# An attention and two-layer kernel: fewer transfers for q, k and v, left over rows placed on both sides

## The chip, the core and the metric

The kernel runs on one core of a Trainium2 chip. The core has five engines that run on their own and meet by semaphores: TensorE (PE; its weight loads are PEld), VectorE (DVE), ScalarE (ACT), GpSimd (POOL) and SyncE (SP), which here only issues transfers. Each engine takes its instructions in order. SBUF and PSUM are the on-chip memories, with 128 partitions; TensorE writes to PSUM only. The metric is the device time of one execution, in microseconds (us).

## The reference, cut to what matters

```python
batch, n_heads, seq, head_dim = (4, 8, 576, 64)
scores = scale * np.matmul(q, k.transpose(0, 1, 3, 2))
thresh = np.max(scores, axis=-1, keepdims=True) - tau
scores = np.where(scores >= thresh, scores, -1000000000.0)
attn = np.exp(scores - np.max(scores, axis=-1, keepdims=True))
attn = attn / (np.sum(attn, axis=-1, keepdims=True) + 1e-09)
x = np.matmul(attn, v)                 # then (2304, 512): tokens by heads
r = np.maximum(x @ w_in, 0.0)          # layer one, 512 -> 2048 -> 512
x = (s * (r * r) + b) @ w_out
h = x @ w2_in                          # layer two, 512 -> 2048 -> 512
out = (h * np.tanh(softplus(h))) @ w2_out
```

All is in float32. There are 32 heads; the kernel takes them as 16 pairs.

## The kernel before, in words

**Attention by pairs.** A pair of heads has 2 x 576 rows of q, k and v. `load_raw` brings them to SBUF: partition p holds rows 4p to 4p+3 of the first 512, as four chunks, and the 64 left over rows lie in a fifth chunk, in half of the partitions. For the second head the order is shifted for k and v, so that its left over rows come first. `prep_qk` transposes the five chunks of both heads at once on TensorE (L204) into a PSUM tile tp; the same tiles hold the scores. ScalarE copies it to `hi` in a rounded format (L208), VectorE makes `lo`, the rest (L209), and `move` brings both to the tiles Q, KH and KL, in which each head owns one half of the partitions and the other half holds the counterpart or zeros (L226; in the first pair engines do it). `hi` and `lo` have one buffer each, so the next hi waits until the moves out of it have landed. Right after the transpositions the raw tile is filled again for the next pair.

A pair's scores come in nine steps: four of head 0, one with the left over rows of both, four of head 1. A step is S (L252), the negated scores and their minimum ns (L256), the threshold (L258), the exponentials e (L263), masking and row sums (L267), scaling (L277). Seven steps later e is transposed (T, L289 to L298), copied to te (L300), and multiplied with v (pv, L311). At a pair's end `split_x` makes xh and xl. The T of the left over columns is made by two ordinary products with 64 columns of the identity (L297, L298).

**The layers.** Layer one (`moe1`) takes the tokens of four pairs as one block. Its products (L403) need weights split in two parts. `split_w` does that by pieces of 256 KB: a load into one of three raw buffers (L57), a scaling on ScalarE (L62), three passes on VectorE (L64 to L66; the last frees the raw buffer), a copy on ScalarE (L69), a subtraction on GpSimd (L70). Two pieces make a unit, of which five fit in the ring; units of block 0 are stored to DRAM (L107), and the other blocks load them whole (L395). Layer two (`moe2`) follows when all attention is done.

**What sets the order.** The program makes attention steps until four pairs are ready, with one step of weight splitting in each twelve. Then `run` hands out steps of attention and of layer one in proportion to what is left of each, attention at a higher priority. A list scheduler with its own model of durations turns this into one order for each engine. SyncE issues nearly all transfers, in that order, and a transfer that waits holds up those behind it.

The lines that the change touches most, of the loads of k and of the moves of q:

```python
nc.sync.dma_start(t[:, 0:4, 0, :], h2[0, 0:512, :].rearrange("(p c) d -> p c d", c=4))
full = h2[1, 64:576, :].rearrange("(p c) d -> p c d", c=4)
nc.sync.dma_start(t[64:128, 0:4, 1, :], full[0:64])
nc.sync.dma_start(t[0:64, 1:5, 1, :], full[64:128])
parts = [(Q, 0, 576, 0)] if h == 0 else [(Q, 0, 512, 704), (Q, 512, 576, 128)]
```

## Time and profile before

| | |
|---|---|
| median of 3 runs | 1206.59 us (1204.57 to 1207.52) |
| profiled execution | 1204.01 us |
| its span, first to last instruction | 1201.8 us |
| PE busy | 1145.2 us, 95% |
| DVE, ACT, POOL busy | 626.1, 529.7, 427.3 us |
| mean granted clock | 0.991 |
| transfers | 161.84 MB, 123667 packets |

The span is one execution on the chip. Busy time is the time in which an engine has an instruction at work; matmuls overlap, so a busy TensorE is not one at its peak. A wait is put down to what came last. Releasers in brackets say what ended an engine's idle time. "issue" is a wait for something that the profile does not show.

### The profile page before, as it was taken

The numbers are of one execution on the slowest core, as the hardware profiler recorded it, in microseconds if no ns is written. First come the engines' busy times: TensorE is split into PE (matmuls) and PEld (weight loads), VectorE is DVE, ScalarE is ACT, GpSimd is POOL, SyncE is SP. The second block draws the span as 40 slices with busy tenths as digits, with TensorE's granted clock in tenths as the row PEclk, the third lists the DMA queues.
The fourth block names the chain that finished last, engine by engine and source line by source line (L and its number), as shares of the span: only waits on it lengthen the run. The fifth ranks groups of instructions, "written<-read, shape, count | busy, mean of one in ns | idle before, by whom it ended". The sixth has DMA issues, their size and how long they took to land.

```text
span 1201.8 us, 19799 instructions
## 1 busy us (share of the span) xinstructions
PE 1145.2 (95%) x7104; PEld 979.2 (81%) x7104; DVE 626.1 (52%) x1505; ACT 529.7 (44%) x1073; POOL 427.3 (36%) x600
## 2 busy tenths in 40 slices
PE   4888999898899999999999999999999999999998
PEld 4666888877678998988988999878888888888886
DVE  5888777878885464655552689964111111111111
ACT  4666666575655544445533465553221221222211
POOL 4566777776644334326422344432000000000000
PEclk8989999999999999999999999999999999999999
DMA  5657466576595455374423898763030020030000
GB/s 128 166 136 183 110 217 184 159 207 173 170 289 156 158 154 159 125 233 140 136 86 106 256 324 283 276 230 105 1 105 1 1 70 1 1 105 1 19 1 35
DMA packets 123667, 161.84 MB, mean 135 GB/s; under 512 B 57393, under 2 KB 78897, under 8 KB 123569
## 3 DMA queue, kind: packets, MB, share of 16 engines
q1 hardware_dynamic: 123568, 160.58, 43.5%
q8 instruction: 56, 0.92, 0.3%
q14 instruction: 43, 0.34, 0.1%
HBM read 107.48 MB, written 30.93 MB: 115 GB/s over the span
## 4 chain that ended last, share of the span: by engine, by line
PE 69%; DMA 10%; DVE 8%; POOL 5%; issue 3%; ACT 2%; SPq 2%; DVEq 0%; ACTq 0%; POOLq 0%
PE o L522 17%; PE h L403 11%; PE y L403 10%; PE hm L493 8%; PE hp L493 8%; PE pv L311 6%; DMA wraw<-in_moe_w_in_dram 4%; PE S L252 4%; DMA wraw<-in_moe_w_out_dram 4%; PE T L289 3%; POOL e L277 3%; DVE wa L64 1%; DMA w<-w 1%; DVE wa L65 1%; DVE wa L66 1%
## 5 line engine op out<-in xcount | busy, mean ns | idle before, releaser
L507 DVE TENSOR_TENSOR g2l<-t,g2h 128x512 fp32r<-128x512 f32 (+1 forms) x80 | 51.9, 648 | 315.4 <-ACT t L506 311.6
L403 PE MATMUL y<-gh,w 128*128 128x288 f32 x768 | 164.6, 300 | 3.1 <-DVE y L450 2.9
L403 PE MATMUL h<-xh,w 128*128 128x288 f32 x768 | 165.5, 301 | 1.9 <-DMA w<-w 1.7
L522 PE MATMUL o<-w2o,g2h 128*128 128x512 f32 x576 | 150.0, 395 | 1.9 <-ACT g2h L505 1.9
L267 DVE SCALAR_TENSOR_TENSOR e<-ns,st,e 128x576 f32<-128x576 f32 x128 | 119.2, 935 | 47.3 <-ACT e L263 33.4
L277 POOL TENSOR_SCALAR e<-e,st 128x576 f32<-128x576 f32 x128 | 127.5, 1005 | 32.3 <-DVE st L272 26.1
L256 DVE TENSOR_SCALAR_CACHE_REDUCE ns<-S 128x576 f32<-128x576 f32 x144 | 107.7, 751 | 54.2 <-PE S L252 53.3
L403 PEld LDWEIGHTS y<-gh,w 128*128 128x128 f32 x768 | 125.8, 188 | 11.1 <-issue 4.4
L403 PEld LDWEIGHTS h<-xh,w 128*128 128x128 f32 x768 | 125.9, 188 | 9.5 <-issue 5.7
L263 ACT ACTIVATE e<-ns,st 128x576 f32<-128x576 f32 x128 | 98.8, 776 | 70.9 <-DVE ns L256 59.6
L522 PEld LDWEIGHTS o<-w2o,g2h 128*128 128x128 f32 x576 | 107.0, 188 | 26.7 <-ACT g2h L505 2.3
L300 ACT COPY te<-T 128x576 f32<-128x576 f32 x144 | 91.1, 632 | 66.6 <-PE T L294 60.5
L258 POOL TENSOR_SCALAR st<-st,tau_c 128x1 f32<-128x1 f32 x144 | 61.1, 426 | 164.9 <-DVE ns L256 140.7
L403 PE MATMUL y<-gl,w 128*128 128x288 f32 x384 | 113.8, 297 | 0.5 <-DVE gl L427 0.5
L252 PE MATMUL S<-KH,Q 128*128 128x288 f32 x320 | 100.3, 329 | 14.6 <-DVE ns L256 5.0
L403 PE MATMUL h<-xl,w 128*128 128x288 f32 x384 | 113.8, 297 | 0.0
L289 PE MATMUL T<-ident,e 128*128 128x128 f32 x576 | 98.3, 279 | 13.8 <-ACT te L300 8.6
L493 PE MATMUL hm<-y,w2i 128*128 128x512 f32 (+1 forms) x480 | 108.4, 372 | 0.0
L493 PE MATMUL hp<-y,w2i 128*128 128x512 f32 (+1 forms) x480 | 107.2, 372 | 0.0
L427 POOL TENSOR_TENSOR gl<-rr,gh 128x288 fp32r<-128x288 f32 x96 | 80.6, 845 | 73.8 <-DVE rr L426 63.2
L311 PE MATMUL pv<-te,rawv 128*64 128x288 f32 x640 | 105.6, 420 | 0.0
L493 PEld LDWEIGHTS hm<-y,w2i 128*128 128x128 f32 x480 | 84.5, 188 | 18.0
(94 smaller groups left out, 2122.7 us busy)
## 6 DMA issues: line engine op xcount, KB each, us to landing
w<-w SPq DMA_DIRECT2D x96, 512.0 KB, 4.2
wraw<-in_moe_w_in_dram SPq DMA_DIRECT2D x64, 256.0 KB, 3.9
w<-wp SPq DMA_DIRECT2D x32, 512.0 KB, 4.0
wraw<-in_moe_w_out_dram SPq DMA_DIRECT2D x64, 256.0 KB, 4.4
KH<-hik SPq DMA_DIRECT2D x60, 144.0 KB, 2.5
y<-yT SPq DMA_DIRECT2D x32, 256.0 KB, 4.0
KL<-lok SPq DMA_DIRECT2D x30, 144.0 KB, 2.7
rawq<-in_q_dram SPq DMA_DIRECT2D x32, 128.0 KB, 3.0
```

Of the source, the lines that this page charges most:

```text
L252: nc.tensor.matmul(so, Q[:, c0:c0 + 128], kt[:, ks], start=(i == 0), stop=(i == len(terms) - 1))
L256: nc.vector.tensor_scalar(ns.rearrange("p (h n) -> p h n", h=2), sv, -0.125, 3.0e38, op0=ALU.mult, op1=ALU.min, accum_out=nm[:, c1])
L263: nc.scalar.activation(e, ns, AF.Exp, bias=nm[:, c1], scale=-1.0)
L267: nc.vector.scalar_tensor_tensor(e, ns, nthr[:, c1], e, op0=ALU.is_le, op1=ALU.mult, accum_out=sm[:, c1])
L277: nc.gpsimd.tensor_scalar(t, t, rinv[:, j:j + 1], u[:, j:j + 1], op0=ALU.mult, op1=ALU.add)
L289: nc.tensor.transpose(T[:, i * 128:i * 128 + 128], self.es[pr, i, "pair"][:, o:o + 128], self.ident)
L300: nc.scalar.copy(te, T[:, :576])
L311: self.nc.tensor.matmul(self.pv[HALVES[h], hf * HB:hf * HB + 288], v[:, h, c, :], tes[h][:, hf * 288:hf * 288 + 288], start=first, stop=last)
L403: nc.tensor.matmul(acc[:, :n], w[:, wl, c], rhs[c][xl][:, ts], start=(i == 0), stop=(i == 11))
L427: (nc.vector if b == 3 else nc.gpsimd).tensor_tensor(gl[:, ts], r2, gh[:, ts].bitcast(F32), op=ALU.subtract)
L493: nc.tensor.matmul(hp[:, :n], w[:, wl, kc, fs], yy[kc], start=(i == 0), stop=(i == 11))
L522: nc.tensor.matmul(outs[t], g[:, t * 128:t * 128 + 128], w[:, wl, fc % 4, :], start=(fc == 0 and i == 0), stop=(fc == 15 and i == 2))
```

## The change

The loads of a pair take 7 transfers: for q and for k one for the first 512 rows of both heads and one for the left over rows, for v one and two. No order is shifted any more. Instead `raw_t` places the transposed left over rows twice in tp, before the other chunks (columns 192 to 256) and behind them (768 to 832), by two ordinary products with 64 columns of the identity; hi and lo are 640 columns wide, head 0 uses the columns from 64 on and head 1 those up to 576. So each move is one piece: 6 for k and 4 for q, 10 in place of 12. In the first pair `prep_first` gives hi and lo of q tiles of their own, copies the parts of head 0 on three engines, and moves those of head 1 by transfers; q's first load is issued on ScalarE. The zeros of the raw tiles are written earlier, and the small constants share one tile.

```diff
@@ -36,11 +36,9 @@
         self.ident, self.swap = i2[:, 0:128], i2[:, 64:192]
         make_identity(nc, self.ident)
         nc.gpsimd.tensor_copy(i2[:, 128:192], i2[:, 0:64])
-        self.tau_c = pool.tile([P, 1], F32, name="tau_c")
-        self.s_c = pool.tile([P, 1], F32, name="s_c")
-        self.b_c = pool.tile([P, 1], F32, name="b_c")
-        self.colsum = pool.tile([P, 4], F32, name="colsum")
-        self.cb = pool.tile([P, 4], F32, name="cb")
+        small = pool.tile([P, 11], F32, name="small")
+        self.tau_c, self.s_c, self.b_c = (small[:, i:i + 1] for i in range(3))
+        self.colsum, self.cb = small[:, 3:7], small[:, 7:11]
 
 
     def split_w(self, src, hi, lo, pool, tags, kw):
@@ -132,6 +130,10 @@
     def attn_alloc(self):
         nc = self.nc
         self.sets = []
+        self.qk = {}
+        for n in "kq":
+            t = self.qk[n] = self.at.tile([P, 5, 2, 64], F32, name=f"raw{n}", bufs=1)
+            nc.gpsimd.memset(t[64:128, 4], 0.0)
 
         e4 = self.at.tile([P, 1344], F32, name="E4", bufs=1)
         for g in range(3):
@@ -146,10 +148,6 @@
             for h in range(2):
                 nc.gpsimd.memset(KL[h][HALVES[1 - h], :].bitcast(F32), 0.0)
             self.sets.append((Q, KH, KL, e4[:, g * 640:g * 640 + 704]))
-        self.qk = {}
-        for n in "qk":
-            t = self.qk[n] = self.at.tile([P, 5, 2, 64], F32, name=f"raw{n}", bufs=1)
-            nc.gpsimd.memset(t[64:128, 4], 0.0)
         self.vs = []
         for g in range(2):
             t = self.at.tile([P, 2, 5, 64], F32, name=f"rawv{g}", bufs=1)
@@ -163,28 +161,19 @@
         if b >= self.B:
             return
         src = {"q": self.q, "k": self.k, "v": self.v}[nm]
+        dma = nc.scalar if nm == "q" and not pr else nc.sync
         h2 = src[b, 2 * p:2 * p + 2]
-        rem = h2[:, 512:576, :].rearrange("h r d -> r h d")
+
+        most = h2[:, 0:512, :].rearrange("h (p c) d -> p c h d", c=4)
         if nm == "v":
             t = self.vs[pr % 2]
+            nc.sync.dma_start(t[:, :, 0:4, :], most.rearrange("p c h d -> p h c d"))
             for h in range(2):
-                nc.sync.dma_start(t[:, h, 0:4, :], h2[h, 64 * h:64 * h + 512, :].rearrange("(p c) d -> p c d", c=4))
-            nc.sync.dma_start(t[0:64, 0, 4, :], h2[0, 512:576, :])
-            nc.sync.dma_start(t[64:128, 1, 4, :], h2[1, 0:64, :])
+                nc.sync.dma_start(t[HALVES[h], h, 4, :], h2[h, 512:576, :])
         else:
             t = self.qk[nm]
-            nc.sync.dma_start(t[:, 0:4, 0, :], h2[0, 0:512, :].rearrange("(p c) d -> p c d", c=4))
-            if nm == "q":
-                nc.sync.dma_start(t[:, 0:4, 1, :], h2[1, 0:512, :].rearrange("(p c) d -> p c d", c=4))
-                nc.sync.dma_start(t[0:64, 4, :, :], rem)
-            else:
-
-
-                full = h2[1, 64:576, :].rearrange("(p c) d -> p c d", c=4)
-                nc.sync.dma_start(t[64:128, 0:4, 1, :], full[0:64])
-                nc.sync.dma_start(t[0:64, 1:5, 1, :], full[64:128])
-                nc.sync.dma_start(t[0:64, 0, 1, :], h2[1, 0:64, :])
-                nc.sync.dma_start(t[0:64, 4, 0, :], h2[0, 512:576, :])
+            dma.dma_start(t[:, 0:4], most)
+            dma.dma_start(t[0:64, 4, :, :], h2[:, 512:576, :].rearrange("h r d -> r h d"))
         self.raws[pr, nm] = t
 
     def s_tile(self, name):
@@ -193,43 +182,64 @@
         pool = self.s2p if self.s2p and self.n_s % 2 else self.sp
         return pool.tile([P, 1024], F32, tag="S", name=name)
 
+    def raw_t(self, pr, n):
+        nc = self.nc
+        raw = self.raws.pop((pr, n))
+        tp = self.s_tile(f"tp{n}{pr}")
+
+        for c, o in ((4, 192), (0, 256), (1, 384), (2, 512), (3, 640), (4, 768)):
+            rows = raw[:, c].rearrange("p h d -> p (h d)")
+            if c < 4:
+                nc.tensor.transpose(tp[:, o:o + 128], rows, self.ident)
+            else:
+                nc.tensor.matmul(tp[:, o:o + 64], rows, self.ident[:, 0:64], start=True, stop=True)
+        self.load_raw(pr + 1, n)
+        return tp
+
+    def parts(self, pr, n, tp, tags):
+        nc = self.nc
+        hi, lo = (self.at.tile([P, 1152 if t == "e" else 640], F32R, tag=t, name=f"{w}{n}{pr}",
+                               bufs=8 if t == "e" else 1)[:, :640] for w, t in zip(("hi", "lo"), tags))
+        nc.scalar.copy(hi, tp[:, 192:832])
+        nc.vector.tensor_tensor(lo, tp[:, 192:832], hi.bitcast(F32), op=ALU.subtract)
+        return hi, lo
+
+    def moves(self, pr, n, h, hi, lo):
+
+
+        Q, KH, KL, _ = self.sets[pr % 2]
+        own, oth = HALVES[h], HALVES[1 - h]
+        cols = slice(64 - 64 * h, 640 - 64 * h)
+        out = []
+        for half, t in ((own, hi), (oth, hi if n == "k" else lo)):
+            dst = KH[h] if n == "k" else Q[:, 640 * h:640 * h + 576]
+            out.append((dst[half, :], t[own, cols]))
+        return out + ([(KL[h][own, :], lo[own, cols])] if n == "k" else [])
+
     def prep_qk(self, pr, n):
 
-
-        nc = self.nc
-        raw = self.raws.pop((pr, n))
-        Q, KH, KL, _ = self.sets[pr % 2]
-        tp = self.s_tile(f"tp{n}{pr}")
-        for c in range(5):
-            nc.tensor.transpose(tp[:, c * 128:c * 128 + 128], raw[:, c].rearrange("p h d -> p (h d)"), self.ident)
-        self.load_raw(pr + 1, n)
-        hi = self.at.tile([P, 576], F32R, tag="hi", name=f"hi{n}{pr}", bufs=1)
-        lo = self.at.tile([P, 576], F32R, tag="lo", name=f"lo{n}{pr}", bufs=1)
-        nc.scalar.copy(hi, tp[:, :576])
-        nc.vector.tensor_tensor(lo, tp[:, :576], hi.bitcast(F32), op=ALU.subtract)
-        for h, (own, oth) in enumerate((HALVES, HALVES[::-1])):
-            for half, t in ((own, hi), (oth, hi if n == "k" else lo)):
-                if n == "k":
-                    parts = [(KH[h], 0, 576, 0)]
-                else:
-                    parts = [(Q, 0, 576, 0)] if h == 0 else [(Q, 0, 512, 704), (Q, 512, 576, 128)]
-                for dst, a, z, o in parts:
-                    self.move(pr, dst[half, a + o:z + o], t[own, a:z], t is hi)
-            if n == "k":
-                self.move(pr, KL[h][own, :], lo[own, :], None)
-
-    def move(self, pr, dst, src, early):
-
-
-        nc = self.nc
-        if pr:
-            nc.sync.dma_start(dst.bitcast(F32), src.bitcast(F32))
-        elif early is None:
-            nc.gpsimd.tensor_copy(dst, src.bitcast(F32))
-        elif early and dst.shape[-1] > 64:
-            nc.scalar.copy(dst, src.bitcast(F32))
-        else:
-            nc.vector.tensor_copy(dst, src.bitcast(F32))
+        hi, lo = self.parts(pr, n, self.raw_t(pr, n), ("hi", "lo"))
+        for h in range(2):
+            for dst, src in self.moves(pr, n, h, hi, lo):
+                self.nc.sync.dma_start(dst.bitcast(F32), src.bitcast(F32))
+
+    def prep_first(self):
+
+
+        nc = self.nc
+        tps = [self.raw_t(0, n) for n in "kq"]
+        (kh, kl), (qh, ql) = (self.parts(0, n, tp, tags) for n, tp, tags in
+                              zip("kq", tps, (("hi", "lo"), ("e", "e"))))
+        k0, k1, k2 = self.moves(0, "k", 0, kh, kl)
+        q0, q1 = self.moves(0, "q", 0, qh, ql)
+        nc.scalar.copy(k0[0], k0[1].bitcast(F32))
+        nc.gpsimd.tensor_copy(k1[0], k1[1].bitcast(F32))
+        nc.gpsimd.tensor_copy(k2[0], k2[1].bitcast(F32))
+        nc.scalar.copy(q0[0], q0[1].bitcast(F32))
+        nc.vector.tensor_copy(q1[0], q1[1].bitcast(F32))
+        for n, hi, lo in (("k", kh, kl), ("q", qh, ql)):
+            for dst, src in self.moves(0, n, 1, hi, lo):
+                nc.sync.dma_start(dst.bitcast(F32), src.bitcast(F32))
 
 
 
@@ -334,8 +344,7 @@
         nc.sync.dma_start(self.s_c, self.s.partition_broadcast(P))
         nc.sync.dma_start(self.b_c, self.b.partition_broadcast(P))
         self.load_raw(0, "v")
-        for n in "kq":
-            self.prep_qk(0, n)
+        self.prep_first()
         fin = todo = None
         tes = {}
         for k in range(N + LAG + 2):
```

Three places of the order that the scheduler makes of it. First ScalarE at the start of the program, before (hik, hiq: the copies to hi of pair 0; KH, Q: the tiles of the scores; e: exponentials; in brackets the semaphores waited for):

```order
L208 CAST hik0_165<-tpk0_154 128x576 [waits PE_49]
L230 CAST KH00_115<-hik0_165 64x576 [waits Activation_49]
L230 CAST KH00_115<-hik0_165 64x576
L230 CAST KH01_116<-hik0_165 64x576 x2
L208 CAST hiq0_184<-tpq0_175 128x576 [waits DVE_49,PE_49,Activation_49]
L230 CAST Q0_113<-hiq0_184 64x576 [waits Activation_49]
L230 CAST Q0_113<-hiq0_184 64x512
L263 ACTIVATE e0_0_203<-ns0_0_200,st0_194 128x576 [waits DVE_49]
L263 ACTIVATE e0_1_213<-ns0_1_210,st0_194 128x576 [waits DVE_49]
```

And with the change (wraw0: the first raw piece of the weights, wp: its split result):

```order
L175 DMA rawq_107<-in_q_dram 128x8x64
L176 DMA rawq_107<-in_q_dram 64x2x64
L203 ACT_TABLE_LOAD
L203 CAST hik0_163<-tpk0_145 128x640 [waits PE_49]
L235 CAST KH00_115<-hik0_163 64x576 [waits Activation_49]
L60 ACTIVATE wraw0_335<-wraw0_335 128x256 [waits DMAHW2_49]
L203 CAST hiq0_167<-tpq0_154 128x640 [waits PE_49]
L238 CAST Q0_113<-hiq0_167 64x576 [waits Activation_49]
L67 CAST wp0_0_0_334<-wa0_337 128x256 [waits DVE_49]
L273 ACTIVATE e0_0_190<-ns0_0_187,st0_181 128x576 [waits DVE_49]
```

The loads of q stand at the head of ScalarE's queue, two moves of KH01 are gone, and the scaling of the first weight piece has come to stand ahead of hiq.

Second, SyncE where pair 8's k is prepared and pair 9's loaded, before (rawk, rawv: loads; hik, lok: the sources of moves; w1: a store of a weight unit):

```order
L186 DMA rawk_131<-in_k_dram 64x64
L176 DMA rawk_131<-in_k_dram 128x4x64
L184 DMA rawk_131<-in_k_dram 64x4x64
L185 DMA rawk_131<-in_k_dram 64x4x64
L187 DMA rawk_131<-in_k_dram 64x64
L226 DMA KH00_115<-hik8_2876 64x576 x2
L226 DMA KL00_117<-lok8_2877 64x576
L226 DMA KH01_116<-hik8_2876 64x576 x2
L226 DMA KL01_118<-lok8_2877 64x576
L172 DMA rawv0_133<-in_v_dram 64x64
L173 DMA rawv0_133<-in_v_dram 64x64
L107 DMA w1_0_2_3_3156<-wp0_2_3_2980 128x1024
```

And with the change (wraw: loads of weight pieces 44 and 45):

```order
L55 DMA wraw44_3182<-in_moe_w_out_dram 128x2x256
L175 DMA rawk_105<-in_k_dram 128x8x64
L176 DMA rawk_105<-in_k_dram 64x2x64
L224 DMA KH00_115<-hik8_2826 64x576 x2
L224 DMA KL00_117<-lok8_2827 64x576
L224 DMA KH01_116<-hik8_2826 64x576 x2
L224 DMA KL01_118<-lok8_2827 64x576
L172 DMA rawv0_129<-in_v_dram 64x64 x2
L105 DMA w1_0_3_0_3176<-wp0_3_0_3023 128x1024
L55 DMA wraw45_3220<-in_moe_w_out_dram 128x2x256
```

Five loads of k have become two, the six moves are as before, and loads of weights stand directly before and close behind.

Third, TensorE in block 0, where output group (2, 1) of layer one is made (y0_2_1_0 and y0_2_1_1 are its two halves, gh and gl the hidden values, wp1_2_1 the weight unit), before, between the scores S8_1 and S8_2:

```order
L403 MATMUL y0_2_1_0_3756<-gh0_2_0_2708,wp1_2_1_3306 128x288
L403 MATMUL y0_2_1_0_3756<-gl0_2_0_2709,wp1_2_1_3306 128x288
L403 MATMUL y0_2_1_1_3803<-gh0_2_0_2708,wp1_2_1_3306 128x290
L403 MATMUL y0_2_1_1_3803<-gl0_2_0_2709,wp1_2_1_3306 128x290
L403 MATMUL y0_2_1_0_3756<-gh0_2_0_2708,wp1_2_1_3306 128x288
L403 MATMUL y0_2_1_0_3756<-gh0_2_1_2817,wp1_2_1_3306 128x288
L403 MATMUL y0_2_1_0_3756<-gl0_2_1_2818,wp1_2_1_3306 128x288
L403 MATMUL y0_2_1_0_3756<-gh0_2_1_2817,wp1_2_1_3306 128x288
L403 MATMUL y0_2_1_1_3803<-gh0_2_0_2708,wp1_2_1_3306 128x290
L403 MATMUL y0_2_1_1_3803<-gh0_2_1_2817,wp1_2_1_3306 128x290
L403 MATMUL y0_2_1_1_3803<-gl0_2_1_2818,wp1_2_1_3306 128x290
L403 MATMUL y0_2_1_1_3803<-gh0_2_1_2817,wp1_2_1_3306 128x290
```

And with the change, between T7_2 and the other half:

```order
L412 MATMUL y0_2_1_0_3699<-gh0_2_0_2660,wp1_2_1_3254 128x288
L412 MATMUL y0_2_1_0_3699<-gl0_2_0_2661,wp1_2_1_3254 128x288
L412 MATMUL y0_2_1_0_3699<-gh0_2_0_2660,wp1_2_1_3254 128x288
L412 MATMUL y0_2_1_0_3699<-gh0_2_1_2769,wp1_2_1_3254 128x288
L412 MATMUL y0_2_1_0_3699<-gl0_2_1_2770,wp1_2_1_3254 128x288
L412 MATMUL y0_2_1_0_3699<-gh0_2_1_2769,wp1_2_1_3254 128x288
L412 MATMUL y0_2_1_0_3699<-gh0_2_2_3203,wp1_2_1_3254 128x288
L412 MATMUL y0_2_1_0_3699<-gl0_2_2_3204,wp1_2_1_3254 128x288
L412 MATMUL y0_2_1_0_3699<-gh0_2_2_3203,wp1_2_1_3254 128x288
L412 MATMUL y0_2_1_0_3699<-gh0_2_3_3292,wp1_2_1_3254 128x288
L412 MATMUL y0_2_1_0_3699<-gl0_2_3_3293,wp1_2_1_3254 128x288
L412 MATMUL y0_2_1_0_3699<-gh0_2_3_3292,wp1_2_1_3254 128x288
```

The twelve products of a half, which stood in pieces of two and four, now stand in one run, ahead of pair 8's scores rather than among them.

## Rows read from the trace of the kernel before

**Rows 1.** Busy us by stretch: PE, PEld, DVE, ACT, POOL; clock, DMA:
```profile
0.00:31.00 31.00, 15.40 (x63) 12.86 (x64) 16.65 (x45) 13.80 (x21) 15.81 (x50) 0.87 0.54 127
31.00:131.00 100.00, 87.69 (x566) 63.98 (x565) 83.06 (x237) 63.15 (x110) 60.70 (x84) 0.94 0.59 158
131.00:354.00 223.00, 206.57 (x1469) 176.29 (x1467) 176.83 (x440) 137.57 (x288) 161.84 (x227) 1.00 0.63 187
354.00:660.00 306.00, 305.26 (x2251) 272.90 (x2252) 162.52 (x393) 145.74 (x271) 121.91 (x172) 1.00 0.49 150
```

**Rows 2.** SyncE's queue, what it waited for, 131 to 354: us, times, longest:
```profile
SPq L57 <- DVE wa L66: 53.1, 21, 6.2
SPq L186 <- PE tpk L204: 12.6, 4, 8.6
SPq L176 <- PE tpq L204: 9.4, 3, 4.0
```

**Rows 3.** Timeline of SyncE's queue, 186 to 204 us: start, us, instruction:
```profile
192.04 0.61 SPq L186 DMA_DIRECT2D rawk<-in_k_dram  x1
...
201.55 1.29 SPq L57 DMA_DIRECT2D wraw<-in_moe_w_out_dram  x2
```

**Rows 4.** Timeline of VectorE, 192.5 to 193.2 us:
```profile
192.19 0.78 DVE L66 SCALAR_TENSOR_TENSOR wa<-wraw,wa 128x256 int32<-128x256 int32 x1
```

**Rows 5.** Timeline of TensorE, 108 to 122 us:
```profile
116.45 0.33 PE L297 MATMUL T<-ident,E 128*128 128x64 f32 x2
116.62 0.39 PE L298 MATMUL T<-ident,E 128*128 128x64 f32 x2
116.84 0.72 PE L204 MATMUL tpq<-ident,rawq 128*128 128x128 f32 x5
```

**Rows 6.** Busy time of line L208 alone by stretch: us, ACT (count):
```profile
131.00:354.00 223.00, 6.33 (x10) 1.00 0.63 187
354.00:660.00 306.00, 6.32 (x10) 1.00 0.49 150
```

**Rows 7.** Timeline of all engines, 0 to 24 us:
```profile
0.72 0.70 SPq L176 DMA_DIRECT2D rawk<-in_k_dram  x1
...
5.32 1.30 PE L204 MATMUL tpk<-ident,rawk 128*128 128x128 f32 x5 [5.32 <-DMA rawk<-in_k_dram]
...
8.09 1.30 PE L204 MATMUL tpq<-ident,rawq 128*128 128x128 f32 x5 [1.47 <-DMA rawq<-in_q_dram]
...
10.07 0.64 ACT L208 CAST hiq<-tpq 128x576 fp32r<-128x576 f32 x1
...
12.36 0.58 PE L252 MATMUL S<-KH,Q 128*128 128x288 f32 x1 [2.97 <-DVE Q L232]
...
18.29 0.43 ACT L62 ACTIVATE wraw<-wraw 128x256 f32<-128x256 f32 x1 [2.05 <-DMA wraw<-in_moe_w_in_dram]
```

**Rows 8.** DMA issues: size and median us from issue to landing:
```profile
wraw<-in_moe_w_in_dram SPq DMA_DIRECT2D x64, 256.0 KB, 3.9
...
rawq<-in_q_dram SPq DMA_DIRECT2D x32, 128.0 KB, 3.0
```

**Rows 9.** VectorE by line, 31 to 131 us: busy us, mean ns, idle:
```profile
L66 DVE SCALAR_TENSOR_TENSOR wa<-wraw,wa 128x256 int32<-128x256 int32 x11 | 5.6, 512 | 0.1
L65 DVE SCALAR_TENSOR_TENSOR wa<-wraw,wa 128x256 int32<-128x256 int32 x11 | 5.0, 456 | 0.0
L64 DVE TENSOR_SCALAR wa<-wraw 128x256 int32<-128x256 int32 x11 | 4.2, 389 | 1.9 <-POOL wp L70 1.3 <-ACT wraw L62 0.5
```

**Rows 10.** ScalarE, what it waited for, 0 to 131: us, times, longest:
```profile
ACT wraw L62 <- DMA wraw<-in_moe_w_in_dram: 6.0, 5, 2.1
...
ACT hiq L208 <- issue: 1.6, 1, 1.6
```

**Rows 11.** Groups of ScalarE and of VectorE, 131 to 354 us:
```profile
L319 ACT CAST xh<-pv 128x576 fp32r<-128x576 f32 x6 | 3.8, 633 | 0.5 <-PE pv L311 0.5
...
L320 DVE TENSOR_TENSOR xl<-pv,xh 128x576 fp32r<-128x576 f32 x6 | 4.5, 748 | 0.4 <-ACT xh L319 0.4
```

More of the change, by code (lines that the diff above doesn't have):

```diff
@@ L194, in s_tile @@
         return pool.tile([P, 1024], F32, tag="S", name=name)
-    def prep_qk(self, pr, n):
+    def raw_t(self, pr, n):
         nc = self.nc
         raw = self.raws.pop((pr, n))
-        Q, KH, KL, _ = self.sets[pr % 2]
-        tp = self.s_tile(f"tp{n}{pr}")
-        for c in range(5):
-            nc.tensor.transpose(tp[:, c * 128:c * 128 + 128], raw[:, c].rearrange("p h d -> p (h d)"), self.ident)
-        self.load_raw(pr + 1, n)
-        hi = self.at.tile([P, 576], F32R, tag="hi", name=f"hi{n}{pr}", bufs=1)
-        lo = self.at.tile([P, 576], F32R, tag="lo", name=f"lo{n}{pr}", bufs=1)
-        nc.scalar.copy(hi, tp[:, :576])
-        nc.vector.tensor_tensor(lo, tp[:, :576], hi.bitcast(F32), op=ALU.subtract)
-        for h, (own, oth) in enumerate((HALVES, HALVES[::-1])):
-            for half, t in ((own, hi), (oth, hi if n == "k" else lo)):
-                if n == "k":
-                    parts = [(KH[h], 0, 576, 0)]
-                else:
-                    parts = [(Q, 0, 576, 0)] if h == 0 else [(Q, 0, 512, 704), (Q, 512, 576, 128)]
-                for dst, a, z, o in parts:
-                    self.move(pr, dst[half, a + o:z + o], t[own, a:z], t is hi)
-            if n == "k":
-                self.move(pr, KL[h][own, :], lo[own, :], None)
@@ new lines, in prep_qk @@
+    def prep_qk(self, pr, n):
+        hi, lo = self.parts(pr, n, self.raw_t(pr, n), ("hi", "lo"))
[3 more added lines that the diff above has]
+    def prep_first(self):
+        nc = self.nc
+        tps = [self.raw_t(0, n) for n in "kq"]
[11 more added lines that the diff above has]
+                nc.sync.dma_start(dst.bitcast(F32), src.bitcast(F32))
```

## The prediction

> **What bounds the kernel now.** I read the busy time by stretch first [rows 1]. Four stretches matter. Up to 31 us one pair of heads starts up; from 31 to 131 us attention runs alone; from 131 to 354 us attention and the first block of layer one share the machine, and that block's weights are split on the way in; from 354 to 660 us attention and blocks 1 and 2 run on weights that are already split. In the last of these TensorE is busy 305.26 of 306 us: what is added there is paid in full. From 131 to 354 it lacks 16.4 us (223 less 206.57), with VectorE at 79%. From 31 to 131 it lacks 12.3 us, VectorE has 83%, and the granted clock is 0.94. So a gain can come only from about 16 us in the third stretch, some of 12 in the second and 15.6 in the first; the rest of the program can only lose.
>
> Next I asked what SyncE's queue waits for from 131 to 354 us [rows 2]: 53.1 us at the weight load (L57) for a raw buffer to be read out, 22.0 us at loads of k and q for the transposes before them. The queue is in order, so the weight loads stand behind the attention's transfers. The timeline shows one such place [rows 3]: VectorE's pass that frees a raw weight buffer ends at 192.97 [rows 4], but the load that reuses a buffer is issued at 201.55, because from 192.04 on five loads of k, six moves and what stands beside them are issued first, some 0.6 us each. There are two such bursts in each pair.
>
> **The change, part by part.** All sums are against the profiled execution: 1204.0 us, span 1201.8. The median of the runs shown is 1206.6, so 2.6 us are added at the end.
>
> *The spare columns on TensorE.* Before, a raw tile of q or k takes five transpositions. Five of them take 0.72 us with the tail of the last, about 0.27 [rows 5], so one costs 0.11. Now four remain, and the left over rows go through two ordinary products with 64 columns of the identity. The trace has this form: the products of T at L297 and L298, each recorded as two instructions. They start at 116.45 and 116.62, and the next work at 116.84: 0.39 us for two. A tile costs 4 x 0.11 + 0.39 = 0.83 us against 0.55: 0.28 us more, on 32 tiles 9.0 us. The copies to hi tell where the tiles lie [rows 6]: ten fall from 354 us on, where TensorE never idles: +2.8 us, paid. Ten fall in the weight stretch: 2.8, half hidden, +1.4. Twelve (3.4 us) fall before, where other engines set the pace; they are in the prologue's term. The bounds: if the two products cost no more than two transpositions, 3.5 us in all; at a fallen clock the difference can be half as much again.
> The Trainium skill, "TensorE: Matmul & The Clock Gate", section Terms, speaks against this part: it says transpose mode is 4 times faster for fp32. By that rule two 64-column products cost as much as four transpositions, 0.44 us, and the sum would be 10.6 us in place of 9.0. The rows say 3.5 times, and they decide.
>
> *Wider copies.* The copy to hi (ScalarE) and the subtraction (VectorE; 0.75 us for the same form in [rows 11]) grow from 576 to 640 columns: about 0.08 us each, 2.7 us of VectorE in all, hidden from 131 us on by its idle fifth, and 1.0 us within the prologue term.
>
> *The weight stretch.* A pair issues 24 transfers before and 17 now. At 0.6 us [rows 3] that is 4.2 us of SyncE's queue, 1.8 of it in each of the two bursts, and over five pairs 21 us by which weight loads stand less behind. The ceiling is TensorE's idle 16.4 us. The built order has drawn on it already: VectorE's second and third passes over the weights before the first score of pair 9 number 128 of 128, against 112, and TensorE's groups of 12 products stand whole where they were cut into pieces of two and four. But weights that come sooner need VectorE sooner: 176.83 us of work there does not fit below about 196 us at 90%, and GpSimd has 161.84. I take less than half of the ceiling: -7 us. The bounds are -16 (all idle time gone) and +5 (TensorE now stands at products placed too early, with attention behind them).
>
> *The prologue.* In the order rows of ScalarE the scaling of the first weight piece stands ahead of hiq. Working it through [rows 7]: the first k load is issued at 0.72 and there are two issues in place of five, but the load is 256 KB, for which the weight loads give 3.9 us against 3.0 for 128 KB [rows 8]. So the transposition of k begins near 5.2 (5.32 before) and that of q right after, at 6.6 in place of 8.09. That is 1.5 us won by the second queue. Then hiq waits: the first weight load is the ninth on SyncE and waits for the first loads' landing, so it is issued near 6.6 and lands 3.0 to 3.9 us later, at 9.6 to 10.5; some 0.4 us of scaling, and hiq starts at 10.0 to 10.9 (10.07 before). Subtraction and one copy on VectorE follow, with a weight pass between: first score at 12.8, against 12.36. Start: +0.4 (from -2, if the weight lands before it is asked for, to +2).
> The weights are also pulled forward. By the first score of pairs 1 to 5 VectorE has done 11, 20, 24, 24, 24 of those passes, against 2, 8, 14, 20, 24. A piece costs 0.39 + 0.46 + 0.51 = 1.36 us there [rows 9], so pair 0 gets 6.1 us more, pair 1 2.0, and pairs 2 to 4 8.2 less: nothing in the sum. What goes is the stall of 1.6 us before hiq, whose tile is held by moves queued behind loads, and some of 6.0 us in which ScalarE stands for a weight [rows 10]. Against it stand the 3.4 us of products and 1.0 of width, half hidden. I take -2, between -6 (half of the 12.3 us that TensorE lacks there) and +4 (pairs 0 and 1 pay and nothing returns).
>
> *The end of attention.* Block 3 now begins among the last products of pair 15: its sums stop at the fourth quarter until xh and xl are made, 0.64 + 0.75 us [rows 11]. Before, eleven whole groups of block 2 stood between. +1.3 (0 to 4).
>
> *At nothing:* transfers of 256 KB land 1 us later, but are issued a pair ahead (20 us and more); without that cover they cost 1 us a pair. The small constants in one tile: every reader waits for the engines it waited for before.
>
> Sum: 2.8 + 1.4 - 7 + 0.4 - 2 + 1.3 = -3.1. That is 1200.9 in the profiled execution, **1203.5** as a median. What a measurement of this kernel can tell from no change is about 0.3%, 3.6 us. This forecast lies within it, and its own range is 1198 to 1209.
>
> **The rivals.**
> *The weights were all that lacked.* The queue is free sooner in every burst, and the whole cuts in TensorE's order come true: -14 in the weight stretch, -5 in the prologue, the rest as above: 2.8 + 1.4 - 14 + 0.4 - 5 + 1.3 = -13.1, so 1193.5. For it: the 8.6 us for which a free buffer waits in [rows 3, 4]. Against it: VectorE at 79 and 83%.
> *The products are paid and nothing comes back* (the other side). Place: the weight stretch. VectorE and GpSimd take over as the bound once loads come sooner, 16 pieces a pair in place of 11; gain there 0, the ten tiles' 2.8 us paid, prologue +1.5, the rest as above: 2.8 + 2.8 + 0.4 + 1.5 + 1.3 = +8.8, so 1215.4. It decides if VectorE is busy over about 88% of the stretch. For it: SyncE's longest wait is for a VectorE pass (L66) [rows 2].
> *Two queues bring nothing*: q's transposition starts where it did, at 8.1. Then the start is still worth +0.4, since hiq waits for the weight; that the change so far doesn't do what it says alters no sum.
>
> **How the numbers follow.** The forecast 0.40, the weights in full 0.32, the products paid 0.28. The first gives faster 0.12, same 0.24, slower 0.04; the second faster 0.31 and same 0.01; the third slower 0.25 and same 0.03. Together: faster 0.43, same 0.28, slower 0.29. The range reaches to both rivals, 1193 to 1215, and leaves their outer halves out.
>
> **What would show it.** Right: score 0 first at 12.3 to 13.3 us, ScalarE's hiq directly behind the first wraw; tpk and tpq taking 0.8 us each in a full stretch; more weight passes before pair 1, and none from pair 3 on until block 0 begins; the first block done earlier than 354 us while attention stands further back; TensorE's idle time there down by about 7 us. Wrong: a prologue longer than 131 us, TensorE idle over 18 us in the weight stretch, or idle time from 354 us on beyond 2 us, where now there is 0.7.

## The result, and the profile after

The changed kernel takes 1213.78 us (median of 9 runs, 1209.26 to 1215.51), the kernel before 1206.06 (9 runs beside them): ratio 1.0061, 95% interval 1.0048 to 1.0074. It is slower by 7.7 us, where the prediction said 3.1 faster. The profiled execution took 1214.44 us, its span is 1212.6 (1204.0 and 1201.8 before).

The busy time by stretch of the changed kernel, with the columns of [rows 1]; the last four rows go on where [rows 1] stops:
```profile
0.00:31.00 31.00, 16.86 (x72) 14.83 (x72) 17.43 (x47) 12.81 (x22) 16.31 (x51) 0.81 0.82 202
31.00:131.00 100.00, 89.94 (x588) 69.09 (x588) 81.13 (x230) 62.65 (x104) 59.33 (x83) 0.90 0.55 142
131.00:354.00 223.00, 208.75 (x1494) 182.64 (x1493) 177.84 (x419) 132.26 (x287) 160.55 (x224) 0.99 0.65 198
354.00:660.00 306.00, 305.06 (x2275) 273.86 (x2274) 167.70 (x413) 147.02 (x268) 118.06 (x173) 1.00 0.50 146
660.00:700.00 40.00, 39.01 (x289) 34.89 (x288) 20.81 (x47) 18.41 (x40) 8.49 (x12) 1.00 0.66 218
700.00:740.00 40.00, 38.26 (x289) 38.02 (x288) 36.17 (x88) 26.01 (x71) 23.53 (x18) 1.00 0.79 263
740.00:780.00 40.00, 35.33 (x242) 32.27 (x242) 36.60 (x88) 21.81 (x59) 20.02 (x21) 1.00 0.77 259
780.00:820.00 40.00, 36.01 (x204) 31.61 (x203) 31.44 (x67) 20.25 (x46) 11.68 (x14) 0.96 0.76 257
```
The same last four stretches of the kernel before, same columns:
```profile
660.00:700.00 40.00, 37.79 (x280) 36.97 (x279) 27.96 (x64) 19.47 (x48) 12.48 (x15) 1.00 0.83 265
700.00:740.00 40.00, 39.75 (x300) 39.55 (x299) 36.60 (x89) 26.23 (x73) 19.33 (x17) 1.00 0.91 308
740.00:780.00 40.00, 38.18 (x279) 36.97 (x278) 37.75 (x89) 22.80 (x62) 18.42 (x20) 1.00 0.79 273
780.00:820.00 40.00, 37.37 (x193) 31.16 (x192) 29.46 (x65) 19.69 (x43) 15.33 (x14) 1.00 0.67 223
```
Up to 660 us TensorE is no idler than before: 14.25 us of idle time in the third stretch, against 16.4. Then, where block 3 runs, it lacks 10.4 us from 700 to 820 (120 less 109.60), against 4.7 before.

Busy time says little about work done, since raw tiles and a fallen clock are busy too. So I counted each product that had begun by a time at what its line takes in a dense stretch (a score product 0.138 us, a layer-one product 0.1376, and so on from the spacing of starts), the raw tiles of q and k left out. Us of work ahead (+) or behind (-) of the kernel before, in the profiled executions:

| Kernel | 131 | 354 | 660 | 700 | 820 | last pv | layer two starts |
|---|---|---|---|---|---|---|---|
| before | 0 | 0 | 0 | 0 | 0 | 655.6 | 792.2 |
| changed | -0.5 | +0.3 | -1.9 | -1.1 | -10.1 | 687.1 | 803.8 |
| e1 before, pace | -0.3 | +5.4 | +7.8 | +10.3 | +0.2 | 674.3 | 790.3 |
| e4 transposed | +2.7 | +9.7 | +10.2 | +11.3 | -3.0 | 675.3 | 792.3 |
| e8 other order | +0.1 | +5.1 | +2.9 | +3.7 | -4.6 | 682.5 | 797.5 |
| e9 changed, 16 deferred | +0.5 | +2.7 | +1.1 | +1.9 | +1.6 | 684.2 | 792.1 |
| e10 before, 16 deferred | -1.0 | -1.1 | -1.0 | +1.1 | +8.3 | 656.4 | 786.3 |
| e13 changed, VectorE relieved | -0.1 | +1.9 | -0.4 | +0.6 | +7.8 | 685.6 | 786.8 |
| e14 before, VectorE relieved | -1.4 | -5.2 | -5.7 | -3.6 | +3.0 | 661.5 | 792.0 |

The row of the changed kernel is the finding: level with the kernel before at 354 us, about 1 us behind at 700, 10 behind at 820, and nothing changes after that. "Last pv" is attention's last score and value product. It comes 31 us later, since TensorE's order has 2322 of the 3072 layer-one products ahead of it, in place of 2106: 216 x 0.1376 = 29.7 us.

In the program the splitting of layer two's weights stands behind attention (behind a.close() in run), and its raw pieces use the buffers of xh and xl. In the kernel before, attention's end is not what holds it: the first loads are issued at 668.55 us, 13 us behind the last pv, when block 2's products with xh and xl are through (SyncE's waits, 655 to 700 us), and the first piece follows in ScalarE's timeline:
```profile
SPq L57 <- PE h L403: 2.5, 3, 1.7
673.09 0.43 ACT L62 ACTIVATE wraw<-wraw 128x256 f32<-128x256 f32 x1 [2.47 <-DMA wraw<-in_moe_w_in_dram]
```
In the changed kernel block 2 is through with xh and xl at 662 us. The first loads are issued behind stores of block 2, 3 us ahead of the last pv, and on ScalarE the first piece stands directly behind the copy of the last pv to xh (SyncE's line, then two of ScalarE):
```profile
683.87 6.72 SPq L55 DMA_DIRECT2D wraw<-in_moe_w_in_dram  x5
687.57 0.64 ACT L329 CAST xh<-pv 128x576 fp32r<-128x576 f32 x1 [1.39 <-PE pv L321]
688.16 0.44 ACT L60 ACTIVATE wraw<-wraw 128x256 f32<-128x256 f32 x1
```
It comes 15.1 us later, 1 us behind the last pv (before, 17.5 us behind it). So VectorE has begun fewer pieces by 700 us; its first pass over them from 660 to 700 us, before and changed (busy us and count, clock, DMA):
```profile
660.00:700.00 40.00, 4.16 (x13) 1.00 0.83 265
660.00:700.00 40.00, 1.70 (x6) 1.00 0.66 218
```
From the first piece to layer two's first product it is 119.1 us before and 115.7 now. In the runs e1 to e4, e8 and e12 below, which split the same pieces there, it is 113.7 to 118.9, though TensorE stands anywhere between 9.8 us behind and 11.3 us ahead of the kernel before at 700 us. What TensorE waits for in the changed kernel from 700 to 820 us, longest first:
```profile
PE y L412 <- DVE gl L436: 3.3, 3, 1.7
PE y L412 <- DVE y L459: 2.7, 3, 1.1
PE h L412 <- DVE y L459: 1.2, 2, 0.8
```
All three are block 3's own operations on VectorE (gl is the low part of the hidden values, y layer one's output), 7.2 of the 10.4 us. VectorE's groups there, busiest first (busy us, mean ns, idle before):
```profile
L63 DVE SCALAR_TENSOR_TENSOR wa<-wraw,wa 128x256 int32<-128x256 int32 x52 | 28.7, 556 | 0.3
L64 DVE SCALAR_TENSOR_TENSOR wa<-wraw,wa 128x256 int32<-128x256 int32 x53 | 25.9, 493 | 0.1
L62 DVE TENSOR_SCALAR wa<-wraw 128x256 int32<-128x256 int32 x51 | 20.3, 400 | 12.6 <-ACT wraw L60 7.7 <-POOL w2o L68 2.3 <-POOL w2i L68 1.9
L435 DVE TENSOR_TENSOR rr<-r 128x288 f32<-128x288 f32 x27 | 14.6, 541 | 0.4 <-ACT r L433 0.4
L436 DVE TENSOR_TENSOR gl<-rr,gh 128x288 fp32r<-128x288 f32 x28 | 13.6, 487 | 0.4
L459 DVE SCALAR_TENSOR_TENSOR y<-y,small,y 128x288 f32<-128x288 f32 x24 | 12.1, 509 | 0.9 <-PE y L412 0.9
```
The three passes of the splitting (74.9 us) stand in one queue with block 3's operations. From 700 to 820 us they take nearly as much in the kernel before (71.9 us): what differs is how much of the splitting is done by then.

### The profile page after: what moved, and what is told of

It reads as the page before. It is cut to its first block, busy times and chain, and to the rows that moved or that the text cites. A ratio compares the mean times of both kernels' runs of the same rounds, so it can differ in the third digit from the quotient of the medians.

```text
span 1212.6 us, 19822 instructions
## 1 busy us (share of the span) xinstructions
PE 1157.3 (95%) x7200; PEld 994.3 (82%) x7200; DVE 634.4 (52%) x1502; ACT 527.9 (44%) x1069; POOL 424.9 (35%) x600
## 4 chain that ended last, share of the span: by engine, by line
PE 68%; DVE 10%; DMA 10%; POOL 4%; ACT 4%; issue 3%; SPq 1%; DVEq 0%; ACTq 0%; POOLq 0%
PE o L531 16%; PE h L412 10%; PE y L412 9%; PE hm L502 8%; PE hp L502 8%; PE pv L321 6%; DMA wraw<-in_moe_w_out_dram 5%; PE S L262 5%; DMA wraw<-in_moe_w_in_dram 4%; PE T L299 4%; DVE wa L62 2%; DVE wa L64 2%; DVE wa L63 1%; DVE e L277 1%; POOL e L287 1%
## 5 line engine op out<-in xcount | busy, mean ns | idle before, releaser
L412 PE MATMUL y<-gh,w 128*128 128x288 f32 x768 | 168.2, 303 | 4.1 <-DVE y L459 2.7
L277 DVE SCALAR_TENSOR_TENSOR e<-ns,st,e 128x576 f32<-128x576 f32 x128 | 118.9, 934 | 50.2 <-ACT e L273 38.7
L268 POOL TENSOR_SCALAR st<-st,small 128x1 f32<-128x1 f32 x144 | 57.2, 398 | 178.1 <-DVE ns L266 159.5
L262 PE MATMUL S<-KH,Q 128*128 128x288 f32 x320 | 101.6, 334 | 10.8 <-DVE ns L266 7.0
```

The lines of the kernel that those rows point to most:

```text
L262: nc.tensor.matmul(so, Q[:, c0:c0 + 128], kt[:, ks], start=(i == 0), stop=(i == len(terms) - 1))
L277: nc.vector.scalar_tensor_tensor(e, ns, nthr[:, c1], e, op0=ALU.is_le, op1=ALU.mult, accum_out=sm[:, c1])
L412: nc.tensor.matmul(acc[:, :n], w[:, wl, c], rhs[c][xl][:, ts], start=(i == 0), stop=(i == 11))
```

## The experiments

Two theories stood at first. A: the order puts layer one ahead of attention, and the late end of attention is paid in block 3. B: the 64-column products cost TensorE time, and nothing else counts.

**e1**, the kernel before with another constant in the merge, which makes its order like the changed one's (2298 products ahead of the last pv):
```
-  ... (a_done - 5000.0) / a_left <= m_done / m_left
+  ... (a_done - 6000.0) / a_left <= m_done / m_left
```


> The kernel before with one constant of the hand-out changed from 5000 to 6000; no transfer, product or move is touched. In the built order this alone puts the layers further ahead of attention: 2298 of 3072 products of layer one stand before the last product of pair 15, against 2106 before and 2322 with the change. Theory A (the change lost its time at the end of attention: attention ends late in the new order, the splitting of layer two's weights starts late, and block 3 becomes bound by VectorE): attention ends 15 to 30 us later than before (655.6), the first load of a layer two weight comes after 675 us instead of 668.5, layer two starts near 800 instead of 792.2, and the time is 1210 to 1214. Theory B (the two 64-column products are paid, 9 us in all, and nothing else matters): 1206, within 2.


1203.15 us, ratio 0.9971 (0.9959 to 0.9984): A's number is refuted, and B's 1206 missed as well. The table says why for A: it was 10.3 us ahead at 700 and lost all of that by 820. The loss that A speaks of is there, and a gain before it, that A didn't have, made up for it.

**e2**, two raw buffers for weights in place of three:
```
-  self.pre, ("raw", "ra"), bufs=3)
+  self.pre, ("raw", "ra"), bufs=2)
```


> The change with two raw buffers in place of three for the weights of layer one; all else as in the change, the 64-column products too. The built order puts fewer products of layer one (2238 in place of 2322) before the last product of pair 15, and layer two's first weight loads ahead of block 2's last stores. Theory A: the weights come slower, the weight stretch idles no less than in the change (14 us) and perhaps 4 more, but block 3 gets its time back, layer two starts near 797 to 800 in place of 803.8, time 1207 to 1211. Theory B: no gain, 1213 to 1217.


1218.15, 1.0105 (1.0077 to 1.0132). A miss: the weights came later (block 1 starts at 357.4, against 333.4), and attention still ended at 685.6.

**e3**, block 3's squares (rr) on GpSimd:
```
-  (nc.vector if b > 0 else nc.gpsimd)
+  (nc.vector if 0 < b < 3 else nc.gpsimd)
```


> The change with the squares of block 3 (rr, 32 operations, 17.9 us on VectorE in the change) computed on GpSimd; the order up to block 3 is the same. Theory A: VectorE is what block 3 waits for (88% busy from 688 to 804 us), so 5 to 10 us come back: layer two starts near 796, time 1204 to 1209. Theory B: 1213 to 1215, as the change.


1214.32, 1.0063 (1.0043 to 1.0083). No gain; layer two starts at 806.0. That speaks against VectorE alone as the cause, but the operation now stands among GpSimd's own part of the splitting.

**e4**, left over rows by two 128-column transpositions:
```
-  nc.tensor.matmul(tp[:, o:o + 64], rows, self.ident[:, 0:64], start=True, stop=True)
+  nc.tensor.transpose(tp[:, o:o + 128], rows, self.ident)
```


> The change with the left over rows transposed twice (128 columns each, of which the next chunk or nothing covers the rest) in place of the two products with 64 columns: 6 transpositions a tile, 0.66 us by the rows of before, in place of 0.83; 32 tiles, 5.4 us of TensorE less. The layers stand as far ahead of attention as in the change. Theory A: at most the share of the dense stretch returns, 0 to 3 us: 1211 to 1214, block 3 as slow as in the change. Theory B: 1208 to 1209.


1203.85, 0.9983 (0.997 to 0.9997): 10 us better, about twice what B allows. Both theories are short of it. This edit also changes the order that the scheduler builds, so it does not price the products alone.

Theory L takes from A what the traces kept: the splitting starts late, and VectorE paces block 3. **e5 to e7** defer the last 8 pieces of layer two's first weights, in the changed kernel, the one before, and e4's:
```
-  w2 = ... (("i", 0), ("o", 0), ("i", 1), ("o", 1), ("i", 2), ("i", 3))
+  w2 = ... (("i", 0), ("o", 0), ("i", 1), ("o", 1), ("i", 2))
-  drain(self.moe2(... (("o", 2), ("o", 3)) ...
+  drain(self.moe2(... (("o", 2), ("i", 3), ("o", 3)) ...
```


> The changed kernel, but the last quarter of layer two's first weights (8 of the 48 pieces of 128x256 that are split beside block 3) is split beside layer two's products instead, where VectorE has room. Theory L (attention ends late, so the splitting of layer two's weights starts late, and VectorE paces block 3): before, after and the three variants start layer two 114 to 119 us after the first of these pieces is scaled; 8 pieces fewer, at 0.40 + 0.56 + 0.48 us of VectorE each and gaps, take 11 to 14 us from this, so layer two starts at 790 to 794 in place of 803.8, with the last score and value products where they were (687), and the time is 1202 to 1205. Theory B (the 64-column products cost TensorE time all through attention, and nothing else differs): TensorE's own work ends no earlier; layer two starts at 802 or later, and the time stays at 1212 to 1215.

> The same deferral in the kernel before. Theory L: here attention ended at 655.6, the first piece was scaled at 673.1, and TensorE lost only 4 us between 750 and 800, so at most 4 us come back: 1201.5 to 1205, and the changed kernel with the deferral stands within 3 us of this one. Theory B: no change, 1204 to 1207, and the changed kernel with the deferral stays 6 to 10 us above it.

> The changed kernel with left over rows by 128-column transposes, and the deferral. Theory L: that kernel had 10 us more of TensorE's products behind it at 700 us than the kernel before and lost them all by 790 in block 3; with the deferral it keeps 8 to 11 of them, layer two starts at 781 to 784, and the time is 1192 to 1197. Theory B: no change from 1203.85, that is 1202 to 1206.


1205.39, 1197.76 and 1194.87 (0.9996, 0.998 to 1.0011; 0.9937, 0.9921 to 0.9953; 0.9905, 0.989 to 0.9921). Splitting less beside block 3 is worth 8 to 9 us in each of the three (the edit moves ScalarE's and GpSimd's parts and the loads as well as VectorE's passes). But the kernel before gains as much as the changed one, twice what L allowed it: the difference between them stays 7.6. Layer two starts 110.6 us behind the last pv in e5, where e13 below, without gaps on TensorE, takes 101, so eight pieces fewer had not freed block 3.

**e8**, the changed kernel's instructions in another order:
```
-  with tc.high_priority(offset=200):
+  with tc.high_priority(offset=0):
```


> The changed kernel with the same instructions in another order: attention's instructions get no head start in priority (0 in place of 200), which gives TensorE nearly the counts of layer-one products between the pairs that the variant with transposes had (648, 1068, 1500, 2088 and 2322 ahead of pairs 5, 8, 10, 12 and the end). It asks how much of the 10 us between the changed kernel and its variant with transposes is order, and how much the products themselves. Theory O (order): by 354 us as much TensorE work is done as in that variant (9 us more than in the changed kernel), and the time is 1204 to 1208. Theory P (the products, by their own 0.14 us for a raw tile and by the lower granted clock before 131 us): 1211 to 1215.


1209.6, 1.0034 (1.0022 to 1.0045): between the two, 4.2 us under the changed kernel. An order nearer to e4's is worth some 4 of e4's 10 us. The other 6 are not parted between the products and the rest of e4's order.

**e9 to e11** defer 16 pieces, in the same three kernels, with TensorE's order as it was:
```
-  w2 = ... (("i", 0), ("o", 0), ("i", 1), ("o", 1), ("i", 2), ("i", 3))
+  w2 = ... (("i", 0), ("o", 0), ("i", 1), ("o", 1))
-  drain(self.moe2(... (("o", 2), ("o", 3)) ...
+  drain(self.moe2(... (("i", 2), ("o", 2), ("i", 3), ("o", 3)) ...
-  for _ in range(2): next(rest, None)
+  for _ in range(3): next(rest, None)
```


> The changed kernel with the last two quarters of layer two's first weights (16 of 48 pieces) split beside layer two's products, three steps of splitting to a product tile there in place of two; TensorE's order is the changed kernel's. The first deferral (8 pieces) took 8 us from the changed kernel and 8 from the kernel before, and left layer two starting 110.6 us after the last score and value product of the changed kernel (132.9 in the kernel before). Theory L, amended (the late end of attention still holds the splitting back with 8 pieces deferred; with 16 it no longer paces block 3): layer two starts at 787 to 791 and the time is 1195 to 1200, within 3 us of the kernel before with the same deferral. Rival N (what separates the two kernels does not hang on the splitting beside block 3): the changed kernel stays 6 to 9 us above the kernel before with the same deferral, at 1201 to 1206.

> The same deferral of 16 pieces in the kernel before, TensorE's order unchanged. Amended theory L: one deferral had already taken away what block 3 lost to VectorE here (4 to 5 us between 700 and 820); a second brings 0 to 3 more: 1195 to 1198. Rival N: the same, so the difference to the changed kernel decides.

> The changed kernel with left over rows by 128-column transposes and 16 pieces deferred. Amended theory L: with one deferral it had 8.5 us more behind it at 700 than the kernel before, but started layer two 109.4 us after attention's last product, gated; with two, layer two starts at 778 to 783 and the time is 1186 to 1191. Rival N: 1192 to 1196, as with one deferral.


1204.22, 1196.93, 1191.77 (0.9974, 0.9958 to 0.9991; 0.9915, 0.9895 to 0.9934; 0.9868, 0.9851 to 0.9886). Amended L missed again for e9, and rival N's numbers came there: the difference is still 7.3 us (e11 lies between the two). But the table places it: e9 and e10 stand 0.8 us apart at 700 and 6.7 at 820. It is still block 3. In e9 TensorE's longest wait there is for a load of layer one's weights (1.8 us), then for gl and y on VectorE (1.6 and 1.2).

**e12**, q of the first pair on SyncE's queue, behind k:
```
-  dma = nc.scalar if nm == "q" and not pr else nc.sync
+  dma = nc.sync
```


> The changed kernel with q of the first pair on SyncE's queue behind k, in place of ScalarE's: one queue for the first loads. Theory Q (the second queue is worth its 3 us in the first score): the first score comes at 14 to 16 us in place of 12.6; of this 0 to 3 us are left at the end, 1212 to 1217. Rival (both queues share what the transfers can move, so that order alone counts): the first score stays within 1 us of 12.6, and the time at 1212 to 1215.


1210.48, 1.0023 (1.001 to 1.0035). Neither expectation: the first score comes sooner, at 10.19. Lines of the timeline of all engines of the changed kernel:
```profile
0.72 0.73 ACTq L175 DMA_DIRECT2D rawq<-in_q_dram  x1
...
6.19 0.66 PE L195 MATMUL tpk<-ident,rawk 128*128 128x64 f32 x2 [6.19 <-POOL gl L426]
...
9.71 0.67 ACT L203 CAST hiq<-tpq 128x640 fp32r<-128x640 f32 x1
...
12.64 0.58 PE L262 MATMUL S<-KH,Q 128*128 128x288 f32 x1 [3.02 <-DVE Q L239]
```
and of e12:
```profile
2.28 0.61 SPq L175 DMA_DIRECT2D rawq<-in_q_dram  x1
...
4.53 0.66 PE L195 MATMUL tpk<-ident,rawk 128*128 128x64 f32 x2 [4.53 <-DMA rawk<-in_k_dram]
...
8.00 0.69 ACT L203 CAST hiq<-tpq 128x640 fp32r<-128x640 f32 x1 [0.20 <-PE tpq L195]
...
10.19 0.50 PE L262 MATMUL S<-KH,Q 128*128 128x288 f32 x2 [2.22 <-DVE Q L239]
```
With two queues k's tile starts 1.7 us later. It waits for its load: the bracket names GpSimd, whose last small writes end at the same time, but in e12 these writes end at 6.0 us too and k's tile has long begun. The first loads alone (DMA issues up to 1.6 us; the last number is the time from issue to landing), in the changed kernel:
```profile
rawk<-in_k_dram SPq DMA_DIRECT2D x1, 256.0 KB, 4.9
```
and in e12:
```profile
rawk<-in_k_dram SPq DMA_DIRECT2D x1, 256.0 KB, 3.5
```
The first score comes 2.4 us sooner in e12. The other 0.7 us are order, not the queue: in e12 the first weight piece is no longer scaled ahead of hiq, and its three passes no longer stand among VectorE's first operations for q, so that from hiq to the first score it is 2.2 us in place of 2.9. The order changes in other places too, so the 3.3 us of time are not the queue's alone.

**e13 and e14** decide the open point, whether VectorE's splitting causes block 3's loss at all. Two of VectorE's three passes over each piece of layer two's weights are left out, in the changed kernel and in the kernel before; TensorE's order in e13 is the changed kernel's, product for product:
```
+  if tags[0] == "raw":
       nc.vector.scalar_tensor_tensor(a, low, 29, a, ...)
       nc.vector.scalar_tensor_tensor(a, high, -0x80000000, a, ...)
```


> The changed kernel without two of VectorE's three operations on each piece of layer two's weights (0.56 and 0.48 us, 64 pieces; the weights of layer two lack their low bits and signs, so its output is wrong): 66 us less of VectorE between attention's end and layer two's first blocks, TensorE's order unchanged. Theory V (in the changed kernel block 3 loses 10 us between 700 and 820 because VectorE's splitting stands ahead of block 3's own evictions): TensorE is without gaps there, layer two starts at 786 to 791, the time is 1196 to 1200, and within 3 us of the kernel before so relieved. Rival S (block 3 loses them by where it starts, right on attention's end, with loads and evictions of its own in its way): layer two starts at 793 or later, and the changed kernel stays 6 to 9 us above the kernel before so relieved.

> The kernel before without the same two operations (layer two's output is wrong). It lost 5 to 8 us to VectorE between 750 and 820, as its two deferrals showed: 1196 to 1199 under both theories; the changed kernel so relieved stands within 3 us of this under V, 6 to 9 us above it under S.


1195.32 and 1196.66 (0.9909, 0.9896 to 0.9922; 0.9924, 0.991 to 0.9937): theory V. The changed kernel's 7.7 us are gone; it now stands 1.3 under the other, the intervals overlapping. Busy time by stretch of e13:
```profile
700.00:740.00 40.00, 40.00 (x304) 40.00 (x304) 25.88 (x59) 30.97 (x86) 21.29 (x28) 1.00 0.97 337
740.00:780.00 40.00, 40.00 (x303) 40.00 (x303) 22.59 (x54) 20.29 (x54) 11.20 (x14) 1.00 0.90 318
780.00:820.00 40.00, 40.00 (x196) 33.62 (x195) 17.16 (x30) 21.55 (x47) 12.97 (x16) 1.00 0.57 180
```
TensorE has no gap in block 3, though attention ends at 685.6 (687.1 in the changed kernel) and block 3's first product starts at 679.0 (680.5). Rival S, that the place of its start is what costs, falls. What the runs don't part is VectorE's own queue from what waits behind it: loads wait for the buffers that VectorE reads out, and relieving it frees these sooner too.

**e15** joins e11's edits and e12's:


> The variant with transposes and 16 pieces deferred, and the first loads on one queue. One queue alone brought the changed kernel's first score from 12.6 to 10.2 us and its time from 1213.8 to 1210.5. Under both theories it adds to the others: 1187 to 1191; if the gain of one queue is lost in the wait for layer one's first weights, 1191 to 1193.


1191.04 (0.9882, 0.9867 to 0.9896), on the border of the two expectations and within the spread of e11's runs (median 1191.77), so what one queue adds here is not shown. It is 15 us under the kernel before and 23 under the changed one.

## Why the prediction was wrong

Its terms against the table (profiled executions, us of the end; a loss is positive):

| Stretch | forecast | measured |
|---|---|---|
| start and prologue, to 131 | 0.4 - 2 = -1.6 | +0.5 |
| weight stretch, 131 to 354 | 1.4 - 7 = -5.6 | -0.8 |
| 354 to 660 | +2.8 | +2.2 |
| end of attention and block 3, to 820 | +1.3 | +8.2 |
| sum | -3.1 | +10.1 (span: +10.8) |

Each measured row is one execution of each kernel, and the medians differ by 7.7 us. Others with TensorE's order unchanged up to 660 us put a row's scatter at some 2 us: from 131 to 354 e5, e9 and e13 win 1.4 to 2.2, e6, e10 and e14 lose 0.1 to 3.8.

**The step that failed most is the end of attention**, +1.3 with a bound of 4, measured at +8.2. I looked at what block 3's first sums wait for (xh and xl), and that was right: 0.7 and 0.3 us in the trace of the changed kernel. I did not ask what else starts at that point. The splitting of layer two's weights does, 15 us later than before, with 6 pieces begun by 700 us in place of 13; the rest shares VectorE with block 3. "Attention stands further back" stands in my own list of what would be right; its price wasn't worked out. The sign was there: my rows stop at 660 us, and from 660 to 820 TensorE lacked 6.9 us in the kernel before, with VectorE busy 36.60 and 37.75 of 40 us in the middle. Before, the last pv had slack, because the splitting waited for block 2 and not for it: with 31 us of delay the first piece came only 15 us later. That the splitting's work on VectorE costs what block 3 lost is shown by e13 and e14. That an earlier start alone would give it back is argued from the pieces begun and the 114 to 119 us; no run starts the splitting sooner with TensorE's order kept.

**The weight stretch** was the other: -0.8 in place of -5.6. The first half of the mechanism came true and the gain did not. The first weights are there sooner, block 0 ends at 333.4 in place of 354.7, but SyncE waits as long as before for VectorE [rows 2], and twice as long for GpSimd (8.8 us before):
```profile
SPq L55 <- DVE wa L64: 51.8, 23, 4.0
SPq L105 <- POOL wp L68: 17.2, 13, 2.5
```
TensorE's idle time there fell by 2.2 us, not 7. Block 0's gain was attention's loss: pair 10's first score came at 388.8, against 353.1. VectorE was busy 177.84 of 223 us (80%), so my rival's condition, over 88%, did not come; its 1215.4 is near the time, but by another mechanism and in another place: that is luck.

**The products** were priced nearly right where TensorE is full. One tile in the changed kernel, TensorE's timeline:
```profile
260.46 0.33 PE L195 MATMUL tpq<-ident,rawq 128*128 128x64 f32 x2
260.63 0.61 PE L193 MATMUL tpq<-ident,rawq 128*128 128x128 f32 x4
261.08 0.33 PE L195 MATMUL tpq<-ident,rawq 128*128 128x64 f32 x2
261.25 0.61 PE L299 MATMUL T<-ident,e 128*128 128x128 f32 x4
```
It takes 0.79 us from first start to the next work; the median of the 20 tiles from 131 us on is 0.78, against 0.545 before and 0.64 in e4. So 0.24 us more a tile, where I had 0.28. One product takes 0.17 us, 1.6 times a transposition of twice the columns: 3.1 times a column. The Trainium skill, "TensorE: Matmul & The Clock Gate", section Terms, gives a factor of 4 for transpose mode in fp32; the rows are below it, and they decide. In the prologue a tile costs more (the first 1.63 us, 6.19 to 7.82, though the granted clock from 5 to 10 us is 1.00). Later in it the granted clock is lower: of the same stretches in e4, whose tiles are transposed,
```profile
0.00:31.00 31.00, 17.03 (x63) 13.92 (x63) 18.97 (x52) 13.08 (x23) 14.72 (x50) 1.00 0.82 206
31.00:131.00 100.00, 91.01 (x598) 68.09 (x598) 81.58 (x232) 64.22 (x105) 62.95 (x87) 0.98 0.56 143
```
the clock is 1.00 and 0.98, against 0.81 and 0.90. That isn't shown to be the products' doing: e7, with e4's order, had 0.76 and 0.94, and e13, with the products, 0.96 and 0.93.

**The start** came as forecast in sum (first score 12.64; 12.8 forecast) with hiq directly behind the first weight's scaling, but partly by luck: k's tile began at 6.19, not 5.2, and q's at 7.82, not 6.6, while the weight was scaled at 9.38, sooner than I had it, just as q's tile was done. The second queue, which I counted as 1.5 us won, cost 1.7 at k's tile (e12).

Left open: why TensorE is 9.4 us further by 354 us in e4 than in the changed kernel, beyond the order's share (e8: 4.8) and 1.4 us of the ten tiles from 131 us on. A part is scatter: e7 and e11, with e4's order up to there, stand at +6.9 and +7.0 in place of +9.7, and e14 at -5.2 with the order of the kernel before.

## What to carry to other kernels

When an order changes, ask of each phase's end which work begins behind it, and which engine then has to do that work beside what: here 31 us of delay to attention cost nothing on TensorE itself up to 700 us and 8 us through VectorE in block 3. A gain of TensorE time ahead of such a gate is given back at it, as e1 and e4 show; deferring the work behind the gate was worth more than the change cost (in the kernel before, 8 us in e6 and 10 in e10). To find such a place, compare the work done by fixed times, since busy time hides it.

## What the runs showed of the hardware

Two 256 KB loads issued at the same time on two queues were no faster than one behind the other: the one that was needed first took 4.9 us in place of 3.5, and what hangs on it came 1.7 us later (e12). The Trainium skill, "DMA: Bandwidth & Descriptors", section Issuing engines are not separate DMA queues, says that both queues end on the same 16 engines; the rows agree. A constant of the merge changed by a fifth (e1) moved 192 products and the time by 3 us: here the order that a scheduler builds is itself a source of differences of some 4 us (e8).
